# Another order of the loading phase in a fused attention and gated-MLP kernel

## The chip, the cores and the metric

The kernel runs on one core of a Trainium2 chip. The metric is the device time of one execution in microseconds (us); the kernel before takes 225.37 us, the median of three runs (225.3 to 225.51).

## What is computed

```python
def _attn_ref(x, state):                       # x (8, 8, 512, 64), state (8, 8, 32, 64)
    scores = scale * np.matmul(x, state.transpose(0, 1, 3, 2))
    a = softmax(scores)                        # over the 32 states
    xread = np.matmul(a, state)
    scores2 = scale * np.matmul(state, x.transpose(0, 1, 3, 2))
    a2 = softmax(scores2)                      # over the 512 tokens
    sread = np.matmul(a2, x)
    return np.concatenate([xread, sread], axis=2)
# then, with heads and depth as 512 features, for all 8 * 544 tokens:
gate = 1.0 / (1.0 + np.exp(-(y @ w_gate)))     # (512, 1536)
val = y @ w_val
return gate * val @ w_out                      # (1536, 512)
```

## The kernel before

The kernel goes through eight batches. For the tokens of a batch it never forms `xread`: it multiplies the state with the weights first (`sw_visit` for batches 0 and 1, `sw_wide` for the others: the products `SW`, for 256, 512 or 768 of the 1536 columns at a time, for the gate with w = 0 and for the value with w = 1, each in two halves e). Then it multiplies the softmax `a`, transposed, with `SW` (`gv_mm(b, f)`: four matmuls for each of the twelve groups f of 128 columns). ScalarE takes the tanh of the gate half (`gv_th`, L298), VectorE joins the two halves (`gv_glu`, L303), and `out_mm` multiplies with `w_out` (twelve calls of four matmuls a batch). Groups f = 0 and 1 need the columns from 0 on, f = 2 and 3 those from 256 on, f = 4 to 7 those from 512 on, and the rest those from 1024 on.

What leads up to `gv_mm(b, ...)` is the attention part. `load_x` brings x of a batch (pieces of two heads, 256 KB each, for batches 0 and 1), `cast_x` turns it into bf16, `xT_mm` and `xT_cp` transpose two heads (four calls j a batch), `S_mm` and `S_exp` give the exponentials of the scores for half a batch i, `n_sum` (a reduction and a reciprocal, L139 and L141) and `n_mul` the normalised softmax, `aT_mm` and `aT_cp` its transpose. `at_Eb` casts the exponentials to bf16 for the other direction, `sr_mm` and `sr_fin` (L218, L226) form `sread` in `XS`. `sT_mm`, `sT_pad` and `sT_cp` transpose the state, `pad` copies the state of batches 2 to 7 into `sTz`. `sw_cp` (L274) moves one half of one `SW` product from the accumulator banks to SBUF. For batches 2 and later x and the softmax are transposed by DMA (`at_xT_dma`, `aT_dma`), issued on SP's queue.

TensorE writes into eight accumulator banks: two of `GV`, four of `SWP`, one each of `OU` and `AT`. A product must wait until its bank's last reader is done.

Weights are loaded by GpSimd's queue (`load_w`, `load_wo`, cast on the way), in which these issues stand in one line with GpSimd's own casts and products (POOL in the profile). x of batches 0 and 1 is issued on SP's queue.

All of batches 0 and 1 is written out by hand, instruction by instruction, as is the start of batch 2: every call adds its instructions to the queues of its engines in the order of the listing, and every engine does its own queue in order. `warm(n, place)` puts n matmuls of constants into TensorE's queue that nobody reads. From batch 2 on a loop over b and f (L654 to L704) does the same in every batch, with `gv_mm(b, f)` and `out_mm(b - 1, f)` in turn and the attention part of the next batch between them. "The loop" below means this one, and its start is the first matmul of `sw_wide(3, 0)`.

Of the kernel before, what the change touches and what calls it, by code (L numbers as in the profile page):

```python
# [16 lines left out]
def kernel(  # L17
# [465 lines left out]
    aT_mm(1, OU)
    sw_cp(1, 0, 2, 0, act)
    sw_cp(0, 0, 2, 1, act)
    gv_th(0, 3)
    gv_mm(0, 2, SWP)
    sw_cp(0, 0, 2, 0, vec)
    gv_mm(0, 0, SWP)
# [248 lines left out]
```

## Time and profile before

| | us |
|---|---|
| median of three runs | 225.37 |
| the profiled execution | 226.03 |
| its span, first to last instruction | 224.2 |
| outside the span | 1.83 |
| TensorE busy | 217.0 (97%) |
| VectorE busy | 140.7 (63%) |
| ScalarE busy | 127.6 (57%) |
| GpSimd busy | 48.8 (22%) |
| granted clock of TensorE | 1.000 |
| first matmul of `gv_mm(0, 3)`, the first of its kind | 16.40 |
| start of the loop | 56.22 |

PE is TensorE, PEld its weight loads, DVE VectorE, ACT ScalarE, POOL GpSimd, SP SyncE. TensorE's busy time counts the `warm` matmuls too (63 of them, all before 9.7 us). A row of the timeline gives the start and the length of a run of like instructions, and in brackets how long the engine had been idle and who released it. A row of the chain gives only the start, the length and the link of the one path that ended last.

### The profile page before, as it was taken

How to read it: one execution, taken by the hardware profiler on the slowest of the kernel's cores; microseconds unless marked ns; L12 is line 12 of the kernel's file. 1: busy time of each engine (PE TensorE's matmuls, PEld its weight loads, DVE VectorE, ACT ScalarE, POOL GpSimd, SP SyncE). 2: the span in 40 equal slices, each digit the busy share in tenths (PEclk: the TensorE clock that was granted, in tenths of full speed). 3: DMA queues.
4: the chain of work that ended last, by engine and by line, in shares of the span. 5: the costliest groups of instructions: out<-in, count | busy, mean ns of one | idle time of the engine just before them, and what ended most of it. 6: DMA issues, size and time to landing. Idle time of an engine off the chain costs nothing.

```text
span 224.2 us, 4791 instructions
## 1 busy us (share of the span) xinstructions
PE 217.0 (97%) x1859; PEld 111.2 (50%) x1859; DVE 140.7 (63%) x248; ACT 127.6 (57%) x239; POOL 48.8 (22%) x85
## 2 busy tenths in 40 slices
PE   7789999999999999999999999999999999999994
PEld 6654444444444545454444454454445444466744
DVE  3599897779368756885488648864787434422311
ACT  2587885645676557656675667556755444423311
POOL 3799560362041004200240006000200000000001
PEclk9999999999999999999999999999999999999999
DMA  6999989753898352627362521253122111111114
GB/s 188 289 201 206 280 130 179 114 193 78 147 292 274 71 151 76 219 59 126 100 225 50 121 96 61 44 81 117 47 78 66 50 50 47 67 73 48 50 26 114
DMA packets 38566, 27.37 MB, mean 122 GB/s; under 512 B 21168, under 2 KB 33840, under 8 KB 38544
## 3 DMA queue, kind: packets, MB, share of 16 engines
q1 hardware_dynamic: 31392, 19.74, 32.5%
q0 software_dynamic: 6864, 7.14, 17.6%
q8 instruction: 14, 0.23, 0.4%
q10 hardware_dynamic: 288, 0.20, 0.3%
q14 instruction: 8, 0.07, 0.1%
HBM read 18.35 MB, written 8.91 MB: 122 GB/s over the span
## 4 chain that ended last, share of the span: by engine, by line
PE 91%; DVE 3%; DMA 2%; ACT 1%; SPq 1%; issue 0%
PE outp L319 38%; PE gvp L288 37%; PE swp L236 5%; PE gvp L291 5%; DMA xf<-in_x_dram 2%; PE srp L213 1%; PE Sp L121 1%; PE outp L339 1%; DVE rs L139 1%; PE srp L210 1%; SPq L74 1%; DVE ab L173 1%; DVE ri L141 0%; DVE r L218 0%; PE xTp L105 0%; PE warm L353 0%
## 5 line engine op out<-in xcount | busy, mean ns | idle before, releaser
L303 DVE SCALAR_TENSOR_TENSOR glu<-th,gvp 128x512 bf16<-128x512 f32 (+1 forms) x108 | 69.9, 655 | 64.0 <-ACT th L298 48.7
L319 PE MATMUL outp<-wo,glu 128*128 128x512 bf16 x396 | 98.2, 379 | 0.0
L288 PE MATMUL gvp<-aT,SW 128*128 128x512 bf16 x384 | 96.3, 379 | 0.3 <-DVE aT L190 0.2
L298 ACT ACTIVATE th<-gvp 128x512 f32<-128x512 f32 (+1 forms) x108 | 61.8, 574 | 60.6 <-PE gvp L288 49.2
L288 PEld LDWEIGHTS <-SW 128*128 128x128 bf16 x384 | 36.3, 98 | 44.7 <-issue 3.1
L319 PEld LDWEIGHTS <-glu 128*128 128x128 bf16 x396 | 37.4, 98 | 40.8 <-issue 0.4
L274 ACT CAST SW<-swp 128x512 bf16<-128x512 f32 x70 | 38.8, 586 | 4.7 <-PE swp L236 3.3
L132 POOL CAST Eb<-E 128x256 bf16<-128x256 f32 x32 | 11.5, 407 | 89.9 <-ACT E L126 89.9
L323 ACT ACTIVATE res<-outp 128x512 f32<-128x512 f32 x33 | 19.7, 597 | 17.6 <-PE outp L319 17.6
L274 DVE CAST SW<-swp 128x512 bf16<-128x512 f32 x26 | 17.1, 683 | 1.6 <-PE swp L236 1.4
L91 POOL CAST xb<-xf 128x1024 bf16<-128x1024 f32 (+1 forms) x13 | 13.8, 1093 | 12.1 <-DMA xf<-in_x_dram 10.7
L330 POOL DMA_DIRECT2D out_dram<-res x2 | 1.1, 542 | 60.0 <-ACT res L323 60.0
L147 DVE TENSOR_REDUCE E<-E 128x128 f32<-128x512 f32 x12 | 12.4, 1035 | 0.0
L139 DVE TENSOR_REDUCE rs<-E 128x16 f32<-128x512 f32 x16 | 10.8, 676 | 1.3 <-ACT E L126 1.3
L126 ACT ACTIVATE E<-Sp 128x512 f32<-128x512 f32 x16 | 9.6, 604 | 2.4 <-PE Sp L121 2.4
L173 DVE TENSOR_TENSOR ab<-E,ri 128x512 bf16<-128x512 f32 x12 | 9.6, 804 | 0.0
L236 PE MATMUL swp<-wg,sTc 64*32 64x512 bf16 (+1 forms) x192 | 8.4, 328 | 0.0
L236 PEld LDWEIGHTS <-sTc 64*32 64x32 bf16 x384 | 4.5, 91 | 7.4 <-issue 4.7
L218 DVE RECIPROCAL r<-srp 128x128 f32<-128x128 f32 x8 | 7.6, 950 | 0.0
L121 PEld LDWEIGHTS <-xT 128*128 128x128 bf16 x128 | 5.5, 98 | 4.0 <-DVE xT L108 1.0
L236 PE MATMUL swp<-wv,sTc 64*32 64x512 bf16 (+1 forms) x192 | 7.4, 322 | 0.0
L291 PE MATMUL gvp<-XS,wg 128*128 128x256 bf16 x48 | 7.2, 273 | 0.0
(64 smaller groups left out, 122.0 us busy)
## 6 DMA issues: line engine op xcount, KB each, us to landing
out_dram<-res SPq DMA_DIRECT2D x31, 256.0 KB, 2.6
xf<-in_x_dram SPq DMA_DIRECT2D x12, 256.0 KB, 4.5
xf<-in_x_dram SPq DMA_DIRECT2D x3, 1024.0 KB, 6.8
wo<-in_moe_w_out_dram POOLq DMA_DIRECT2D x3, 512.0 KB, 5.9
wg<-in_moe_w_gate_dram POOLq DMA_DIRECT2D x2, 512.0 KB, 9.2
wv<-in_moe_w_val_dram POOLq DMA_DIRECT2D x2, 512.0 KB, 10.8
xf<-in_x_dram POOLq DMA_DIRECT2D x2, 512.0 KB, 10.4
xf<-in_x_dram POOLq DMA_DIRECT2D x1, 1024.0 KB, 9.2
```

The lines of the kernel that those rows point to most:

```text
L91: cp(xbs[b].rearrange("p c h d -> p h c d")[:, lo:lo + n], xfs[b][:, lo:lo + n])
L139: nc.vector.tensor_reduce(rs, halfE(b, i), AX.X, ALU.add)
L147: nc.vector.tensor_reduce(held["E4", b][:, e].rearrange("p j n -> p (j n)"), E1s[b][:, :, e].rearrange("p c j n -> p (j n) c"), AX.X, ALU.add)
L173: eng.tensor_tensor(abs_[b].rearrange("p c e (j n) -> p (c e) j n", n=Ns)[:, ce, 2 * i:2 * i + 2], halfE(b, i)[:, ce], ri[:, ce].unsqueeze ...
L236: nc.tensor.matmul(pss[e][j * Ns:(j + 1) * Ns, o:o + n], sTc[rows, b, j] if b > 1 else sTz[rows, b, j, e], (wg, wv)[w][rows, j, lo:lo + n] ...
L274: cp(*sw_left.pop((b, lo, w, e)))
L288: nc.tensor.matmul(ps, SWs[b][:, g, w, fs], aTs[b][:, :, g], start=(g == 0), stop=(g == 1))
L291: nc.tensor.matmul(ps, (wg, wv)[w][:, j, fs], XS[:, j], start=(j == 0), stop=(j == 3))
L298: nc.scalar.activation(th, held["gv", b, f][0], AF.Tanh, scale=0.5)
L303: nc.vector.scalar_tensor_tensor(glus[b][:, f], held["th", b, f], 1.0, held["gv", b, f][1], ALU.add, ALU.mult)
L319: nc.tensor.matmul(ops[b, c], glus[b][:, f, c * 128:(c + 1) * 128], wo[:, f], start=(f == 0), stop=(f == NF - 1))
L323: nc.scalar.activation(res, ops[b, c], AF.Copy, scale=0.5)
```

## The change

The two `load_x` of batches 0 and 1 at the head become one; x of batch 1 is loaded by `load_xp`, one piece each at its place in the listing, in the order 3, 2, 0, 1. `hold(1, i)` lets GpSimd write one element of piece i before that, so that the piece's load has a write of GpSimd to wait for. Batch 0 is taken from head 0 on: the scores of heads 0 to 3 (i = 0) come before those of heads 4 to 7, where before it was the other way round. The first five `load_w` stand in GpSimd's queue directly behind its casts of the state and of x's first piece; the last three come behind its casts of batch 1. `at_Eb` is split by quarters over VectorE, ScalarE and GpSimd, the casts of x are shared out anew, `n_sum` is split into its two instructions, and the number of `warm` matmuls goes from 63 to 85. The first `gv_mm`, the `sw_visit` and everything up to the loop stand in another order; the loop is the same.

The listing of the new order runs up to the loop, several calls to a line; that of the old one up to the fourth `gv_mm`.

```diff
@@ -73,6 +73,18 @@
         for i in range(parts):
             eng.dma_start(xf[:, n * i:n * i + n], v[:, n * i:n * i + n])
+    def load_xp(b, i):
+
+        if b not in xfs:
+            xfs[b] = stg.tile((128, H, 4, D), FP, name="xf")
+        nc.sync.dma_start(xfs[b][:, 2 * i:2 * i + 2], x[b].rearrange("h (p c) d -> p h c d", c=4)[:, 2 * i:2 * i + 2])
+
+    def hold(b, i):
+
+        if b not in xfs:
+            xfs[b] = stg.tile((128, H, 4, D), FP, name="xf")
+        nc.gpsimd.memset(xfs[b][:, 2 * i, 0, 0:1], 0.0)
+
     def load_w(w, lo, n):
         src = (moe_w_gate, moe_w_val)[w].rearrange("(k p) n -> p k n", p=128)
         nc.gpsimd.dma_start((wg, wv)[w][:, :, lo:lo + n], src[:, :, lo:lo + n])
@@ -120,25 +132,37 @@
             for c in range(4):
                 nc.tensor.matmul(ps[:, c, :, jj], xTs[b][:, 2 * i + jj, c], sTz[:, b, 2 * i + jj], start=True, stop=True)
-    def S_exp(b, i):
+    def S_exp(b, i, lo=0, n=4):
         if b not in E1s:
             E1s[b] = ap_.tile((128, 4, 2, 4, Ns), FP, name="E1")
-        nc.scalar.activation(E1s[b][:, :, :, 2 * i:2 * i + 2].rearrange("p c e j n -> p (c e) j n"),
-                             held["S", b, i].rearrange("p c e j n -> p (c e) j n"), AF.Exp, scale=scale)
+        nc.scalar.activation(halfE(b, i)[:, 2 * lo:2 * lo + 2 * n],
+                             held["S", b, i][:, lo:lo + n].rearrange("p c e j n -> p (c e) j n"), AF.Exp, scale=scale)
+
+    def Eb_c(b, c, cp):
+        if b not in Ebs:
+            Ebs[b] = ap_.tile((128, 4, 2, 4, Ns), BF, name="Eb")
+        cp(Ebs[b][:, c], E1s[b][:, c])
     def at_Eb(b):
-        Ebs[b] = ap_.tile((128, 4, 2, 4, Ns), BF, name="Eb")
         for c in range(4):
-            nc.gpsimd.tensor_copy(Ebs[b][:, c], E1s[b][:, c])
+            Eb_c(b, c, pool)
     def halfE(b, i):
         return E1s[b][:, :, :, 2 * i:2 * i + 2].rearrange("p c e j n -> p (c e) j n")
+    def n_red(b, i, lo=0, n=4):
+        if ("rs", b, i) not in held:
+            held["rs", b, i] = ap_.tile((128, 8, 2), FP, name="rs", bufs=4)
+        nc.vector.tensor_reduce(held["rs", b, i][:, 2 * lo:2 * lo + 2 * n], halfE(b, i)[:, 2 * lo:2 * lo + 2 * n], AX.X, ALU.add)
+
+    def n_rec(b, i, lo=0, n=4):
+        if ("ri", b, i) not in held:
+            held["ri", b, i] = ap_.tile((128, 8, 2), FP, name="ri", bufs=4)
+        nc.vector.reciprocal(held["ri", b, i][:, 2 * lo:2 * lo + 2 * n], held["rs", b, i][:, 2 * lo:2 * lo + 2 * n])
+
     def n_sum(b, i):
-        rs = ap_.tile((128, 8, 2), FP, name="rs")
-        nc.vector.tensor_reduce(rs, halfE(b, i), AX.X, ALU.add)
-        ri = held["ri", b, i] = ap_.tile((128, 8, 2), FP, name="ri")
-        nc.vector.reciprocal(ri, rs)
+        n_red(b, i)
+        n_rec(b, i)
     def n_tok(b, e):
@@ -390,266 +414,285 @@
     sbs = {}
     load_s(0, nc.scalar)
-    load_x(0, nc.sync, 4)
-    load_x(1, nc.sync, 4)
     make_identity(nc, ident)
...
-    nc.vector.memset(sTz, 0.0)
...
+    load_x(0, nc.sync, 4)
+    nc.vector.memset(sTz, 0.0)
...
-   cast_x(0, pool, 0, 2); warm(12, OU); cast_x(0, vec, 2, 2); warm(16, GV); warm(8, OU); cast_s(0, pool)
-   load_w(1, 256, 256); sT_mm(0, OU); sT_pad(0, 1, vec); cast_x(0, act, 6, 2); xT_mm(0, 1, SWP); xT_mm(0, 0, AT)
-   cast_x(0, act, 4, 2); sT_pad(0, 0, vec); warm(15, GV); xT_mm(0, 3, OU); xT_cp(0, 0, vec); load_w(0, 256, 256)
-   warm(3, GV); xT_mm(0, 2, SWP); xT_cp(0, 1, vec); xT_cp(0, 2, vec); xT_cp(0, 3, act); warm(3, GV)
-   load_w(0, 0, 256); cast_x(1, vec, 2, 2); warm(6, GV); gate(xfs[0][:, 7, 0, 0:1]); S_mm(0, 1, SWP, (0,))
-   S_mm(0, 1, OU, (1,)); S_mm(0, 0, OU, (0,)); load_w(1, 0, 256); cast_x(1, act, 0, 2); S_mm(0, 0, AT, (1,))
-   S_exp(0, 1); cast_x(1, vec, 4, 2); n_sum(0, 1); load_w(0, 512, 512); S_exp(0, 0); xT_mm(1, 0, SWP)
-   xT_mm(1, 1, SWP); cast_x(1, pool, 6, 2); at_Eb(0); xT_mm(1, 2, AT); xT_cp(1, 2, vec); n_sum(0, 0)
-   xT_mm(1, 3, OU); xT_cp(1, 3, act); S_mm(1, 1, GV); load_sb(2); xT_cp(1, 0, act); S_exp(1, 1); xT_cp(1, 1, vec)
-   S_mm(1, 0, AT); n_mul(0, 1, nc.vector); n_mul(0, 0, nc.vector); n_sum(1, 1); sw_visit(0, 256, 256); sr_mm(0, OU)
-   S_exp(1, 0); sw_cp(0, 256, 2, 1, act); aT_mm(0, AT); sw_visit(1, 256, 256); sw_cp(0, 256, 2, 0, act)
-   aT_cp(0, 0, act); n_sum(1, 0); sw_visit(1, 0, 256); aT_cp(0, 1, vec); load_w(0, 1024, 512); load_w(1, 512, 512)
-   load_w(1, 1024, 512); n_mul(1, 1, nc.gpsimd); sr_fin(0); sw_cp(1, 0, 2, 1, vec); sw_cp(1, 256, 2, 1, act)
-   gv_mm(0, 3, GV); sw_cp(1, 256, 2, 0, act); sw_visit(0, 0, 256); n_mul(1, 0, nc.gpsimd); aT_mm(1, OU)
-   sw_cp(1, 0, 2, 0, act); sw_cp(0, 0, 2, 1, act); gv_th(0, 3); gv_mm(0, 2, SWP); sw_cp(0, 0, 2, 0, vec)
-   gv_mm(0, 0, SWP); aT_cp(1, 0, vec); gv_th(0, 2); gv_glu(0, 3); gv_mm(0, 1, GV); gv_th(0, 0); gv_glu(0, 2)
-   sT_mm(2, AT); aT_cp(1, 1, vec); gv_glu(0, 0); sw_visit(1, 512, 512, 0); gv_th(0, 1); gv_glu(0, 1)
...
+   warm(16, GV); warm(14, OU); hold(1, 1); cast_x(0, vec, 2, 2); hold(1, 2); hold(1, 3); cast_s(0, pool)
+   sT_mm(0, AT); sT_pad(0, 0, act); sT_pad(0, 1, act); cast_x(0, pool, 0, 2); warm(6, GV); xT_mm(0, 0, SWP)
+   cast_x(0, vec, 4, 2); xT_mm(0, 1, SWP); warm(7, GV); xT_mm(0, 2, GV); xT_cp(0, 1, vec); load_w(0, 256, 256)
+   xT_cp(0, 0, act); load_xp(1, 3); S_mm(0, 0, SWP, (0,)); S_mm(0, 0, AT, (1,)); S_exp(0, 0); cast_x(0, vec, 6, 2)
+   xT_cp(0, 2, vec); load_w(1, 256, 256); warm(3, GV); xT_mm(0, 3, AT); xT_cp(0, 3, vec); n_red(0, 0)
+   load_xp(1, 2); n_rec(0, 0); cast_x(1, act, 6, 2); S_mm(0, 1, SWP, (0,)); warm(5, GV); S_mm(0, 1, OU, (1,))
+   S_exp(0, 1); n_red(0, 1); xT_mm(1, 3, OU); load_w(0, 0, 256); load_w(1, 0, 256); load_w(0, 512, 512)
+   xT_cp(1, 3, act); Eb_c(0, 0, vec); Eb_c(0, 1, vec); n_rec(0, 1); n_mul(0, 1, nc.vector); cast_x(1, pool, 4, 2)
+   warm(6, GV); xT_mm(1, 2, SWP); load_xp(1, 0); cast_x(1, pool, 0, 2); warm(7, GV); xT_mm(1, 0, GV)
+   xT_cp(1, 2, act); Eb_c(0, 3, act); S_mm(1, 1, GV); S_exp(1, 1); n_red(1, 1); n_rec(1, 1); Eb_c(0, 2, pool)
+   sr_mm(0, OU); xT_cp(1, 0, vec); load_xp(1, 1); cast_x(1, pool, 2, 2); xT_mm(1, 1, SWP); xT_cp(1, 1, act)
+   n_mul(0, 0, nc.gpsimd); load_w(1, 512, 512); load_w(0, 1024, 512); load_w(1, 1024, 512); aT_mm(0, AT)
+   aT_cp(0, 0, act); aT_cp(0, 1, vec); warm(6, GV); sw_visit(0, 256, 256); sw_cp(0, 256, 2, 1, vec)
+   sw_visit(1, 256, 256); sw_cp(1, 256, 2, 1, vec); sw_cp(0, 256, 2, 0, act); S_mm(1, 0, GV); S_exp(1, 0)
+   warm(7, AT); gv_mm(0, 3, GV); Eb_c(1, 0, pool); n_red(1, 0); sw_cp(1, 256, 2, 0, act); warm(8, SWP)
+   sw_visit(0, 0, 256); n_rec(1, 0); gv_th(0, 3); gv_glu(0, 3); sw_cp(0, 0, 2, 0, act); sw_cp(0, 0, 2, 1, vec)
+   sr_fin(0); sw_visit(1, 0, 256); gv_mm(0, 2, GV); sw_cp(1, 0, 2, 0, act); gv_mm(0, 0, SWP); gv_th(0, 2)
+   gv_glu(0, 2); n_mul(1, 1, nc.gpsimd); gv_th(0, 0); n_mul(1, 0, nc.gpsimd); aT_mm(1, AT); aT_cp(1, 0, vec)
+   gv_glu(0, 0); sw_cp(1, 0, 2, 1, act); Eb_c(1, 3, act); aT_cp(1, 1, vec); gv_mm(0, 1, GV); gv_th(0, 1)
+   gv_glu(0, 1); sw_visit(1, 512, 512, 0); sw_cp(1, 512, 0, 0, act); load_x(2, nc.gpsimd, 2)
+   sw_cp(1, 512, 0, 1, act); sw_visit(0, 512, 512, 0); sw_cp(0, 512, 0, 1, vec); sw_cp(0, 512, 0, 0, act)
+   gv_mm(1, 3, SWP); load_sb(3); gv_th(1, 3); gv_glu(1, 3); Eb_c(1, 1, pool); gv_mm(1, 0, GV); gv_th(1, 0)
+   p_tok(1); gv_glu(1, 0); sw_visit(1, 512, 512, 1); sw_cp(1, 512, 1, 1, vec); sw_cp(1, 512, 1, 0, act)
+   gv_mm(1, 2, SWP); gv_th(1, 2); gv_glu(1, 2); gv_mm(1, 7, GV); load_sb(1); gv_th(1, 7); gv_glu(1, 7)
+   Eb_c(1, 2, pool); sw_visit(1, 1024, 512, 0); sw_cp(1, 1024, 0, 0, vec); sw_cp(1, 1024, 0, 1, act)
+   sw_visit(0, 1024, 512, 0); sw_cp(0, 1024, 0, 0, act); gv_mm(1, 1, GV); gv_th(1, 1); sr_mm(1, OU)
+   sw_visit(1, 1024, 512, 1); sw_cp(1, 1024, 1, 1, act); sw_cp(0, 1024, 0, 1, vec); sw_cp(1, 1024, 1, 0, act)
+   sw_visit(0, 1024, 512, 1); gv_mm(1, 6, GV); gv_glu(1, 1); sw_cp(0, 1024, 1, 0, vec); sw_cp(0, 1024, 1, 1, act)
+   sr_fin(1); gv_mm(1, 10, SWP); gv_th(1, 10); gv_glu(1, 10); gv_th(1, 6); gv_mm(0, 10, SWP); gv_th(0, 10)
+   gv_glu(1, 6); gv_glu(0, 10); gv_mm(1, 4, SWP); gv_th(1, 4); gv_mm(0, 11, GV); cast_x(2, act, 0, 4); gv_glu(1, 4)
+   sw_visit(0, 512, 512, 1); gv_th(0, 11); gv_glu(0, 11); sT_mm(1, SWP); sT_cp(1, act); load_sb(2)
+   sw_cp(0, 512, 1, 1, act); sT_mm(2, AT); sT_cp(2, vec); load_wo(0); cast_x(2, pool, 4, 4); at_xT_dma(2)
+   load_wo(1); sT_mm(3, OU); sw_cp(0, 512, 1, 0, act); gv_mm(1, 11, SWP); gv_th(1, 11); gv_mm(0, 9, GV)
+   gv_th(0, 9); gv_glu(0, 9); gv_mm(1, 5, SWP); gv_glu(1, 11); gv_th(1, 5); sT_cp(3, act); gv_mm(0, 7, GV)
+   gv_th(0, 7); gv_glu(0, 7); gv_glu(1, 5); gv_mm(0, 5, SWP); gv_mm(1, 8, GV); gv_th(0, 5); gv_th(1, 8)
+   gv_glu(0, 5); gv_glu(1, 8); gv_mm(0, 4, SWP); gv_th(0, 4); gv_glu(0, 4); gv_mm(1, 9, GV); gv_th(1, 9)
+   gv_glu(1, 9); gv_mm(0, 8, SWP); gv_th(0, 8); gv_glu(0, 8); gv_mm(0, 6, GV); gv_th(0, 6); gv_glu(0, 6); pad(2, 6)
+   S_mm(2, 0, SWP); S_exp(2, 0); n_red(2, 0); S_mm(2, 1, GV); S_exp(2, 1); n_rec(2, 0); sw_wide(2, 0)
+   out_mm(0, 7, GV); sw_cp(2, 0, 2, 1, act); sw_cp(2, 0, 0, 0, act); out_mm(0, 0, GV); out_mm(0, 9); sw_wide(2, 1)
+   out_mm(0, 2); load_wo(2); load_x(3, nc.gpsimd); out_mm(0, 1, AT); n_red(2, 1); sw_cp(2, 0, 0, 1, act)
+   n_rec(2, 1); n_mul(2, 1, nc.vector); sw_cp(2, 0, 1, 0, act); gate(xTs[2][:, 0, 3, 0:1]); sw_cp(2, 0, 2, 0, vec)
+   sw_cp(2, 0, 1, 1, act); n_mul(2, 0, nc.gpsimd); out_mm(0, 6, OU); aT_dma(2); at_Eb(2); cast_x(3, pool, 0, 4)
+   cast_x(3, pool, 4, 4); sw_cp(2, 1, 0, 1, vec); sw_cp(2, 1, 0, 0, act); at_xT_dma(3); sw_cp(2, 1, 1, 0, act)
+   out_mm(0, 3); n_tok(2, 0); out_mm(0, 8); sw_cp(2, 1, 2, 1, act); n_tok(2, 1); n_split(2, 0); out_mm(0, 5)
+   load_x(4, nc.sync); out_mm(0, 10); sw_cp(2, 1, 2, 0, act); n_split(2, 1); sr_mm(2, SWP); sw_cp(2, 1, 1, 1, act)
+   sr_fin(2); out_mm(0, 4); out_mm(0, 11)
```

More of the change, by code (lines that the diff above doesn't have):

```diff
@@ L479 @@
-    gv_mm(0, 3, GV)
-    sw_cp(1, 256, 2, 0, act)
-    sw_visit(0, 0, 256)
-    n_mul(1, 0, nc.gpsimd)
[L483 to L489, printed above, removed]
+    warm(16, GV)
+    warm(14, OU)
+    hold(1, 1)
+    cast_x(0, vec, 2, 2)
+    hold(1, 2)
+    hold(1, 3)
+    cast_s(0, pool)
+    sT_mm(0, AT)
+    sT_pad(0, 0, act)
+    sT_pad(0, 1, act)
+    cast_x(0, pool, 0, 2)
+    warm(6, GV)
@@ new lines @@
+    n_red(1, 1)
+    n_rec(1, 1)
+    Eb_c(0, 2, pool)
+    sr_mm(0, OU)
+    xT_cp(1, 0, vec)
+    load_xp(1, 1)
+    cast_x(1, pool, 2, 2)
+    xT_mm(1, 1, SWP)
+    xT_cp(1, 1, act)
+    n_mul(0, 0, nc.gpsimd)
+    load_w(1, 512, 512)
+    load_w(0, 1024, 512)
+    load_w(1, 1024, 512)
+    aT_mm(0, AT)
+    aT_cp(0, 0, act)
+    aT_cp(0, 1, vec)
+    warm(6, GV)
+    sw_visit(0, 256, 256)
+    sw_cp(0, 256, 2, 1, vec)
+    sw_visit(1, 256, 256)
+    sw_cp(1, 256, 2, 1, vec)
+    sw_cp(0, 256, 2, 0, act)
@@ L505 @@
[L505 to L523 removed]
+    sw_cp(0, 512, 0, 1, vec)
+    sw_cp(0, 512, 0, 0, act)
+    gv_mm(1, 3, SWP)
@@ L580 @@
     gv_th(1, 4)
[L581 to L590 removed]
+    gv_mm(0, 11, GV)
+    cast_x(2, act, 0, 4)
+    gv_glu(1, 4)
+    sw_visit(0, 512, 512, 1)
+    gv_th(0, 11)
+    gv_glu(0, 11)
+    sT_mm(1, SWP)
+    sT_cp(1, act)
+    load_sb(2)
+    sw_cp(0, 512, 1, 1, act)
+    sT_mm(2, AT)
+    sT_cp(2, vec)
+    load_wo(0)
+    cast_x(2, pool, 4, 4)
```

375 lines of the change are left out of this document (179 added, 196 removed).

## Prediction

> **What bounds the kernel now.** I read the shares of busy time first, then the chain of waits, then the timelines of TensorE and VectorE over the first 60 us, and last the DMA queues in the stretch in which x lands. The page's chain names TensorE for 91% of the span, so a change in the loading phase is worth what it does to the start of the loop: behind it TensorE has no idle time that a different past could fill.
>
> ```profile
> PE 91%; DVE 3%; DMA 2%; ACT 1%; SPq 1%; issue 0%
> ...
> 2.27 5.24 DMA xf<-in_x_dram
> 7.53 0.63 ACT xb L91
> ...
> 16.03 0.32 DVE aT L190
> 16.35 0.88 DVE r L218
> ...
> 18.50 2.62 PE gvp L288 x12
> ...
> 56.29 0.77 PE swp L236 x32
> ```
>
> In the chain, the last piece of x of batch 0 lands at 7.51. From there the path runs over ScalarE and then nearly without a break over VectorE to 17.85, then over TensorE to the end. The timeline of TensorE gives the two marks that I use:
>
> ```profile
> 16.40 1.02 PE L288 MATMUL gvp<-aT,SW 128*128 128x512 bf16 x4 [0.18 <-DVE aT L190]
> 18.34 2.78 PE L288 MATMUL gvp<-aT,SW 128*128 128x512 bf16 x12
> 21.05 0.32 PE L374 MATMUL stp<-ident,sb 128*64 128x64 bf16 x8
> ```
>
> The first gv_mm starts at 16.40, the fourth is done at 21.05, and from there to the loop's start at 56.22 no wait for another engine of more than 0.1 us is listed. Those 35.2 us are pure TensorE work, and the kernel after has the same work there. So its loop starts at (end of its fourth gv_mm) + 35.2 + (new waits).
>
> **Prices.** From the timelines: 12 matmuls of gv_mm in 2.62, so 0.87 for a gv_mm; two sw_visit of 512 columns in 0.83; ScalarE moves a bank in 0.60 alone and 0.53 in a row, VectorE in 0.64; a glu takes 0.64, the reduction and the reciprocal of n_sum 0.68 and 0.25, sr_fin 1.5 (the two rows here). TensorE's result reaches the next engine 0.2 to 0.25 us after its last matmul was issued (S_mm left TensorE at 9.88, ScalarE began at 10.09), and a result of ScalarE or VectorE reaches TensorE after 0.06.
>
> ```profile
> 16.27 0.95 DVE L218 RECIPROCAL r<-srp 128x128 f32<-128x128 f32 x1
> 17.25 0.59 DVE L226 TENSOR_TENSOR XS<-srp,r 64x128 bf16<-64x128 f32 x2
> 17.88 1.29 DVE L274 CAST SW<-swp 128x512 bf16<-128x512 f32 x2
> 19.52 1.28 DVE L303 SCALAR_TENSOR_TENSOR glu<-th,gvp 128x512 bf16<-128x512 f32 x2
> 27.96 1.07 ACT L274 CAST SW<-swp 128x512 bf16<-128x512 f32 x2 [0.20 <-PE swp L236]
> ```
>
> **x of batch 1 released by pieces: nothing.** GpSimd is idle from 1.30 to 4.22, so its three one-column writes (rows of such writes: 0.09 each) are done by 1.6. SP needs 0.5 per issue and comes to batch 1's first piece at 2.7. The new wait has been met by then; behind it only the other three pieces are queued. All eight pieces are issued when they were before, batch 1's in another order. I keep the landings: batch 0's last at 7.53, batch 1's at about 8.3, 9.0, 9.7 and 10.36 (first and second worked out from the median of 5.4 us to landing of these eight, the last from GpSimd's row).
>
> **Five weight loads ahead: nothing.** They leave GpSimd from 4.85 to 8.6 instead of 5.12 to 9.17. But the engines are not free for them:
>
> ```profile
> q1 hardware_dynamic: 1333, 1.28, 94.6%
> q0 software_dynamic: 90, 0.05, 8.9%
> ```
>
> This is the DMA view from 5 to 9 us: 1333 packets of x (q1), 90 of weights (q0), with four weight loads issued. Weights begin to flow when x is through, near 9, at 200 GB/s, and keep that rate to 24; so each load lands by its place in the line. The two of 256 columns that come first land by 12.9, the fourth at 15.9 (TensorE's row of a wait for wv at 15.92), the last of the eight near 26. Walked below, they are asked for at 13.8, 16.9 and 28.7: no wait. If that cover went, 1 us of lateness of the fourth load would cost about 1 us. The last three loads stand behind GpSimd's casts and its n_mul (1.04) and go out from 12.3 instead of 13.1: nothing either, by the same line. The Trainium skill's page "DMA: Bandwidth & Descriptors", section "Queues, rings and completion order", says that an engine takes packets in turn from the queue rows that have work. By that rule loads issued 0.27 earlier would take half of that, 0.13 us, from x's last piece, and the sum would be 0.13 higher; the 1333 packets against 90 do not agree with it.
>
> **The chain to the first gv_mm.** From 7.53 VectorE casts batch 0's last piece (0.54), copies two transposes (8.43; TensorE transposes heads 6 and 7 between; 8.95) and sums heads 0 to 3 (9.88). ScalarE has S_exp(0, 1) done at 10.05, then two copies of transposes (10.55, 11.1), a quarter of Eb (11.45) and S_exp(1, 1) (12.4). The casts of Eb on VectorE and ScalarE are not in the trace; the nearest rows are 0.28 (L165, VectorE, same shape) and 0.37 (L377, ScalarE), bounds 0.25 and 0.6; VectorE has 0.4 us spare there, ScalarE none, so its one can cost -0.1 to +0.25. TensorE does sr_mm(0) to 12.5, the last transposes and aT_mm(0) to 13.3; ScalarE copies to 14.1, VectorE follows to 14.55 and moves one half of each of the first two sw_visit (15.2, 15.85). gv_mm(0, 3) starts at 15.35, 1.05 earlier than before. Its second half waits for S_exp(1, 0), whose bank it takes (15.7), and it ends at 16.2.
>
> **From there to the fourth gv_mm.** Before, sw_visit(1, 0) came ahead of the first gv_mm; now it comes behind, with sw_visit(0, 0) and eight warm matmuls: 17.45. gv_mm(0, 2) and (0, 0) follow to 19.2, aT_mm(1) to 19.7. VectorE has meanwhile n_sum(1, 0), a glu, one SW half and sr_fin(0) in its queue, to 19.65, and the glu that frees the bank for gv_mm(0, 1) ends at 20.3. The fourth gv_mm ends at 20.8. The lead has shrunk from 1.05 to 0.25.
>
> **New waits up to the loop**, each a bank not yet read:
> - sw_visit(0, 512) for glu(0, 0), which stands behind aT_cp on VectorE (21.35): 0.15.
> - gv_mm(1, 3) takes the two banks of sw_visit(1, 512); ScalarE moves them from 21.45 to 22.55 (2 x 0.55) and TensorE is there at 21.75: 0.3 + 0.1. Before, gv_mm(1, 0) in other banks stood at this place.
> - gv_mm(1, 7) for the SW half that VectorE moves last: 0.05; gv_mm(1, 4) for th(0, 10): 0.15.
> - S_mm(2, 1) for th(0, 6), sw_wide(2, 0) and (2, 1) for single banks: 0.15, 0.05 and 0.1.
>
> Sum 1.05. Against the lead of 0.25 the loop starts 0.8 us later, at 57.0. The other gv_mm come in turn in GV and SWP with th and glu shorter than 0.87, so they hide theirs. The extra warm matmuls (22 at 0.067, as 15 in 1.00) lie in stretches where TensorE waits anyway, but for the eight in front of sw_visit(0, 0), 0.5, which are in the walk.
>
> **The sum.** The profiled execution is 224.2 + 1.83 = 226.03 and lies 0.66 over the median 225.37. I add the shift to the median: 225.37 + 0.8 = 226.2 (for a profiled execution like that of before, 226.8). A measurement of this kernel can tell about 0.2%, 0.45 us, from no change.
>
> **Rivals.**
> 1. Faster: VectorE catches up. All waits above but the one for th(0, 10) go back to VectorE and ScalarE being 0.2 to 0.6 us behind TensorE from 19 to 22.5, and the bounds of my walk are of that size. If the walk is 0.35 too slow up to the first gv_mm and VectorE reaches sr_fin(0) 0.4 earlier as well, the lead stays at 0.6 and no wait is left: 224.8. For it: the first gv_mm really starts earlier. Against: VectorE is over 95% busy from 11 to 24 us already now, and TensorE has 0.85 more in front of its fourth gv_mm. It decides if the glu of (0, 2) ends before 19.7. Chance 0.17.
> 2. No change: the hold does hold. If batch 1's pieces stayed out of x's way, batch 0's four (1.05 MB at 345 GB/s) would land near 6.5, and the chain would run 0.9 earlier, until it meets the weight load at 15.9: 225.3. Against: the idle GpSimd row. With what the forecast's own spread puts there, chance 0.16.
> 3. Slower still: x of batch 3 comes late. pad waits for sT_cp(3), which ScalarE now does near 38.3; behind pad (1.72) GpSimd issues load_wo(2) and load_x(3), at 40.9 instead of 40.14. It lands 9.7 later as now, the casts take 2.03, the four transposes of SP 6.16, and the last lands 2.2 later: 61.4. The loop asks for them 4.24 after its start (before, 60.46 against 56.22), at 61.2. That is on the edge, and the forecast counts nothing for it. Every later landing costs its full amount; with 1 us, 227.2. It decides if load_x(3) goes out after 41. Chance 0.17.
>
> **How the numbers follow.** Forecast 0.50, rivals 0.17, 0.16, 0.17. Slower by over 0.45 us: forecast and the third, 0.67; within: 0.16; faster: 0.17. The forecast's own range is 225.8 to 227.2 (waits of half or twice their size, the ScalarE cast's bounds). The whole range goes from the first rival, 224.7, to the third with doubled waits, 227.2 + 0.7 = 227.9.
>
> **What would show it.** In the profile after: SP's eight issues of x without a gap; weights landing as before; gv_mm(0, 3) near 15.4 and the fourth gv_mm ending near 20.8; idle gaps in TensorE's rows ahead of gv_mm(0, 1) and gv_mm(1, 3), released by VectorE and ScalarE; the loop's start near 57.0. It is wrong if the loop starts before 56 or if TensorE stands still for over 0.5 us at any place not named here.

## The result

The kernel after takes 227.10 us (median of 13 runs, 225.72 to 228.35), the kernel before beside it 225.45 (13 runs, 225.17 to 226.16): 1.0067 times as long, 95% interval 1.0042 to 1.0092. Forecast: 226.2 in a range from 224.7 to 227.9, slower with a chance of 0.67. Sign and range held, the time lies inside the forecast's own range of 225.8 to 227.2 too; the size, 0.8, was about half of the 1.65 that was measured.

The first thing to see is that the two profiled executions cannot simply be subtracted: 226.19 for after is among its shortest, 226.03 for before among its longest, and they differ by 0.16 us where the medians differ by 1.65. So the rows below show what the kernel after does in one of its shorter executions, not the whole of what it loses. The page's chain and TensorE's timeline of after, as in the prediction for before:

```profile
PE 91%; DVE 3%; DMA 2%; issue 1%; SPq 1%; ACT 1%
```

```profile
15.15 1.03 PE L312 MATMUL gvp<-aT,SW 128*128 128x512 bf16 x4
...
20.18 0.59 PE L312 MATMUL gvp<-aT,SW 128*128 128x512 bf16 x2 [0.28 <-DVE glu L327]
20.70 0.81 PE L260 MATMUL swp<-wg,sTz 64*32 64x512 bf16 x16
21.82 1.51 PE L312 MATMUL gvp<-aT,SW 128*128 128x512 bf16 x6 [0.30 <-ACT SW L298]
...
56.36 0.41 PE L260 MATMUL swp<-wg,sTc 64*32 64x512 bf16 x8
```

In this execution nearly all is where the prediction put it: the first gv_mm at 15.15 (forecast 15.35), the fourth done at 20.70 (20.8), the wait for VectorE's glu before gv_mm(0, 1), the wait for ScalarE's SW half before gv_mm(1, 3). The loop starts at 56.36 (57.0). The loads, too, do what was said. SP's issues of x follow each other without a gap, and from 5 to 9 us the engines carry 1305 packets of x (q1) and 44 of weights (q0):

```profile
0.74 1.99 SPq L74 DMA_DIRECT2D xf<-in_x_dram  x4
2.78 2.00 SPq L80 DMA_DIRECT2D xf<-in_x_dram  x4
```

```profile
q1 hardware_dynamic: 1305, 1.26, 99.3%
q0 software_dynamic: 44, 0.02, 4.2%
```

The chain over the start shows one thing that the prediction did not have, two VectorE links longer than they were priced: two casts of Eb in 0.82, priced at 0.28 each, and n_mul, the row that writes `ab`, in 1.27 instead of 0.65:

```profile
9.92 0.69 DVE rs L156
10.60 0.82 DVE Eb L144 x2
11.42 0.17 DVE ri L161
11.61 1.27 DVE ab L197
```

### The profile page after: what moved, and what is told of

The parts are those of the page before. It is cut to its first block, busy times and chain, and to the rows that moved or that the text cites. A ratio compares the mean times of both kernels' runs of the same rounds, so it can differ in the third digit from the quotient of the medians.

```text
span 224.4 us, 4813 instructions
## 1 busy us (share of the span) xinstructions
PE 217.2 (97%) x1857; PEld 112.8 (50%) x1881; DVE 139.1 (62%) x240; ACT 131.7 (59%) x249; POOL 49.2 (22%) x84
## 4 chain that ended last, share of the span: by engine, by line
PE 91%; DVE 3%; DMA 2%; issue 1%; SPq 1%; ACT 1%
PE outp L343 37%; PE gvp L312 37%; PE swp L260 5%; PE gvp L315 5%; DMA xf<-in_x_dram 2%; PE Sp L133 2%; PE srp L237 1%; PE outp L363 1%; PE srp L234 1%; PE warm L377 1%; SPq L74 1%; DVE glu L327 1%; DVE ab L197 1%; DVE r L242 0%; DVE Eb L144 0%
## 5 line engine op out<-in xcount | busy, mean ns | idle before, releaser
L343 PE MATMUL outp<-wo,glu 128*128 128x512 bf16 x372 | 95.0, 379 | 1.1
L298 ACT CAST SW<-swp 128x512 bf16<-128x512 f32 x76 | 42.0, 587 | 4.2 <-PE swp L260 2.8
L144 POOL CAST Eb<-E 128x256 bf16<-128x256 f32 x28 | 10.8, 426 | 92.2 <-ACT E L138 92.2
L103 POOL CAST xb<-xf 128x1024 bf16<-128x1024 f32 (+1 forms) x15 | 15.1, 1033 | 6.0 <-DMA xf<-in_x_dram 6.0
L298 DVE CAST SW<-swp 128x512 bf16<-128x512 f32 x20 | 13.5, 684 | 0.4 <-PE swp L260 0.2
L197 DVE TENSOR_TENSOR ab<-E,ri 128x512 bf16<-128x512 f32 x12 | 10.4, 869 | 0.1
L377 PE MATMUL warm<-ones 128*128 128x128 bf16 x85 | 8.2, 259 | 1.0 <-DVE ones L420 1.0
```

The source lines that it names most:

```text
L103: cp(xbs[b].rearrange("p c h d -> p h c d")[:, lo:lo + n], xfs[b][:, lo:lo + n])
L144: cp(Ebs[b][:, c], E1s[b][:, c])
L197: eng.tensor_tensor(abs_[b].rearrange("p c e (j n) -> p (c e) j n", n=Ns)[:, ce, 2 * i:2 * i + 2], halfE(b, i)[:, ce], ri[:, ce].unsqueeze ...
L298: cp(*sw_left.pop((b, lo, w, e)))
L343: nc.tensor.matmul(ops[b, c], glus[b][:, f, c * 128:(c + 1) * 128], wo[:, f], start=(f == 0), stop=(f == NF - 1))
```

## The experiments

Marks of every profiled execution, in us: the first gv_mm; the end of the fourth (start of the next row on TensorE); the start of the loop; what lies behind it to the end of the span; and how long after the loop's start SP issues the first store of the loop's results. Ratios are to the kernel before, measured beside it on the same chip. e1 to e4, e5 to e8, e9 to e11 and e12 ran on four different chips, so across these groups it is the ratios that compare.

| kernel | median | ratio, 95% interval | first gv_mm | fourth done | loop | behind | store |
|---|---|---|---|---|---|---|---|
| before, first profile | 225.45 | 1 | 16.40 | 21.05 | 56.22 | 168.0 | 2.14 |
| before, again | one run, 225.02 | | 15.81 | 20.26 | 55.20 | 168.0 | 2.13 |
| after, first profile | 227.10 | 1.0067, 1.0042 to 1.0092 | 15.15 | 20.70 | 56.36 | 168.0 | 1.26 |
| after, again (e1) | 227.78 | 1.0104, 1.0072 to 1.0136 | 15.79 | 21.34 | 57.00 | 168.0 | 1.47 |
| e3 before's start | 226.48 | 1.0045, 1.0025 to 1.0065 | 16.11 | 20.75 | 56.34 | 168.7 | 1.97 |
| e4 after's start | 227.29 | 1.0076, 1.0053 to 1.0099 | 15.80 | 21.36 | 56.74 | 169.1 | 1.56 |
| e5 Eb off VectorE | 226.25 | 1.0036, 1.0015 to 1.0056 | 15.09 | 20.65 | 56.24 | 168.2 | 1.49 |
| e6 n_mul on VectorE | 226.01 | 1.0029, 1.0004 to 1.0054 | 14.77 | 20.33 | 55.92 | 168.0 | 1.43 |
| e7 no hold | 227.78 | 1.0120, 1.0076 to 1.0163 | 15.95 | 21.51 | 57.17 | 168.9 | 2.35 |
| e8 both of e5, e6 | 226.26 | 1.0040, 1.0019 to 1.0061 | 14.58 | 20.13 | 55.72 | 168.4 | 1.64 |
| e9 behind gv_mm only | 226.53 | 1.0048, 1.0030 to 1.0065 | 15.47 | 20.39 | 56.60 | 168.4 | 1.79 |
| e10 e6 and e9 | 226.66 | 1.0051, 1.0028 to 1.0074 | 14.72 | 19.65 | 55.79 | 169.1 | 2.78 |
| e12 e10, VectorE relieved | 225.79 | 1.0006, 0.9992 to 1.0021 | 14.84 | 19.76 | 55.40 | 169.0 | 2.51 |

**Both kernels again (e1, e2), unchanged.**

> The kernel after once more, unchanged, for a second profiled execution and more times. Theory A (the loading phase itself scatters: landings of x or of weights reach TensorE unhidden, so slow executions lose time ahead of the fourth gv_mm): if this profiled execution is over 226.7 us, its fourth gv_mm ends later than the 20.70 us of the first profile by most of the excess. Theory B (the bank waits between the fourth gv_mm and the loop are what scatters): the fourth gv_mm ends near 20.7 in a slow execution too, and the loop starts later than 56.4. Theory C (the loop itself loses: x of batch 3 or the clock of TensorE): the loop starts near 56.4 and the excess lies behind it, or the granted clock falls below 1. Times: 225.7 to 228.4, median near 227.1, in all three.

> The kernel before once more, for a second profiled execution: its first one took 226.03 us, 0.58 over the median of its runs. All theories: a time of 225.2 to 226.2; if it is near 225.4, first gv_mm and loop start stand up to 0.6 us earlier than the 16.40 and 56.22 of the first profile, which then were late ones.

The two spans now differ by 1.8 us (225.0 and 223.2), all of it ahead of the loop. This execution of before, at 225.02 a little under what was expected, has x's last piece of batch 0 about 1 us earlier than the first one had (its cast begins at 6.51 instead of 7.53). e1 took 227.04, 0.85 more than the first profile of after, and 0.64 of that stands at the end of the fourth gv_mm. That is the place that theory A names, but not its reason: x's last piece is cast from 7.13 on in e1 and from 7.25 in the first profile, and no wait for a weight is listed. Instead sr_mm(0), the product that writes `srp`, stands still; the waits of TensorE, then VectorE's and GpSimd's timelines of e1:

```profile
PE srp L234 <- DVE Eb L144: 1.1, 1, 1.1
```

```profile
9.75 0.69 DVE L156 TENSOR_REDUCE rs<-E 128x16 f32<-128x512 f32 x1
10.35 2.13 DVE L144 CAST Eb<-E 128x256 bf16<-128x256 f32 x2
12.41 0.24 DVE L161 RECIPROCAL ri<-rs 128x16 f32<-128x16 f32 x1
12.68 0.69 DVE L197 TENSOR_TENSOR ab<-E,ri 128x512 bf16<-128x512 f32 x1
```

```profile
10.12 0.44 POOL L144 CAST Eb<-E 128x256 bf16<-128x256 f32 x1
10.47 0.65 POOL L103 CAST xb<-xf 128x512 bf16<-128x512 f32 x1
11.05 1.07 POOL L197 TENSOR_TENSOR ab<-E,ri 128x512 bf16<-128x512 f32 x1
12.05 0.81 POOL L90 DMA_DIRECT2D wv<-in_moe_w_val_dram  x1
```

Of the two casts of Eb on VectorE the one took 1.93 us and the other 0.28. The long one ends at 12.28, 0.16 behind the end of GpSimd's row of three instructions, when only weight issues are left; n_mul behind it then takes its normal 0.69. The profiles of e7 and e9, further down, repeat this: a cast of 2.16 that ends 0.16 behind the end of GpSimd's n_mul, and one of 2.47 that ends 0.17 behind it. In the first profile of after it was the other way round: the casts 0.90 for both, and n_mul, beside GpSimd's own n_mul, 1.26. For comparison VectorE's products and GpSimd's work in the first profile of before, where the casts of Eb are all GpSimd's and over before VectorE's products begin:

```profile
13.03 1.28 DVE L173 TENSOR_TENSOR ab<-E,ri 128x512 bf16<-128x512 f32 x2
```

```profile
11.23 1.44 POOL L132 CAST Eb<-E 128x256 bf16<-128x256 f32 x4 [0.23 <-ACT E L126]
...
13.13 0.75 POOL L78 DMA_DIRECT2D wg<-in_moe_w_gate_dram  x1
13.86 1.50 POOL L78 DMA_DIRECT2D wv<-in_moe_w_val_dram  x2
```

What it costs when an instruction of VectorE is caught, that is, made longer by GpSimd's, can be counted from the start of VectorE's second reduction, n_red(0, 1), to the first gv_mm: 5.23 in the first profile of after, where n_mul was caught, 6.04, 6.26 and 6.58 in e1, e7 and e9, where a cast was, and 5.24 to 5.42 in the profiles of e6, e10 and e12, where GpSimd's n_mul is gone. So a cast that is caught for the whole row costs 0.6 to 1.0 us in e1 and e7 (in e9 VectorE came to it early and stood still for longer), and n_mul caught as in the first profile costs nothing that shows.

**One half of the change each (e3, e4).** e3 has before's order up to the fourth gv_mm and after's from there to the loop; e4 the reverse.

```diff
 e3: the calls up to gv_glu(0, 1) from the kernel before (without load_sb(2), sT_mm(2)), the rest from after
     (with Eb_c(1, 0) and Eb_c(1, 3) on GpSimd, which after has further ahead)
 e4: the calls up to gv_glu(0, 1) from the kernel after (with load_sb(2)), the rest from before
```

> The order of before up to the fourth gv_mm (with state load and transpose of batches 4 and 5 left to the later place), then the order of after up to the loop. Theory A (loading phase): 225.3 to 225.9, and little scatter like before's. Theory B (bank waits behind the fourth gv_mm, +0.5 to +1.05 us): 226.0 to 226.6. Theory C (x of batch 3 issued later, a part of this half): above 226.5 with the scatter of after.

> The order of after up to the fourth gv_mm (with one 64 KB state load added behind GpSimd's product), then the order of before up to the loop. Theory A (loading phase): 226.5 to 227.2 with runs spread over 2 us, like after. Theory B: 225.0 to 225.3, since the start alone is 0.25 to 0.35 us ahead by the walk and by the profile. Theory C: 225.0 to 225.4.

Each half costs time, after's start (e4) more than after's rest (e3). e3 is where theory B puts it, e4 0.1 us over the range of theory A. e4 shows the wait of TensorE for VectorE's Eb that e1 has, at 0.8 us instead of 1.1. e3 loses 0.4 to 0.65 us between the fourth gv_mm and the loop (35.59, before 35.17 and 34.94) and 0.7 behind the loop's start. e4 loses 1.1 there. Its last 16 us ran at a granted clock of 0.97 (0.99 and 1.00 in after and before), by an estimate from these figures 0.3 to 0.5 us of that; what the rest was stays open.

**What VectorE and GpSimd do to each other (e5, e6, e8), and the named parts undone (e7).** Theory A: VectorE's casts and products from SBUF to SBUF (the chip's on-chip memory) stand still while GpSimd's instructions run. Theory B: the scatter comes from the landing of x.

```diff
 e5 (e8 has this and e6)
-    Eb_c(0, 0, vec)
-    Eb_c(0, 1, vec)
...
-    Eb_c(0, 3, act)
+    Eb_c(0, 0, act)
+    Eb_c(0, 1, act)
...
     Eb_c(0, 2, pool)
+    Eb_c(0, 3, pool)
 e6
     n_mul(0, 1, nc.vector)
+    n_mul(0, 0, nc.vector)
...
-    n_mul(0, 0, nc.gpsimd)
 e7
-    hold(1, 1)
-    hold(1, 2)
-    hold(1, 3)
...
+    gate(xfs[0][:, 7, 0, 0:1])
     load_w(1, 0, 256)
     load_w(0, 512, 512)
```

> The kernel after, with the two casts of Eb that stand on VectorE (Eb_c(0, 0) and Eb_c(0, 1)) given to ScalarE, and ScalarE's own (0, 3) to GpSimd. Theory A (VectorE's casts from SBUF to SBUF stand still while GpSimd's instructions run: 0.28 us where GpSimd is idle, 1.93 in one execution): no wait of TensorE for VectorE's Eb any more, sr_mm(0) starts at 11.2 to 11.6, but n_mul(0, 1) on VectorE still meets GpSimd's n_mul(0, 0) (1.26 instead of 0.65); first gv_mm at 15.1 to 15.4 in every execution, the median 0.3 to 0.8 us below the kernel after as it was run twice (227.10, 227.78), so 226.5 to 227.0, with less scatter. Theory B (the scatter comes from the landing of x's pieces): median 227.1 to 227.8 and the same scatter of 2 us; the first gv_mm moves with the landing.

> The kernel after, with n_mul(0, 0) moved from GpSimd to VectorE, behind n_mul(0, 1). Theory A: GpSimd has no long instruction left between its cast of x at 10.5 and its weight issues, so a VectorE cast that was caught behind both of GpSimd's instructions is now caught behind the cast alone, and is done by 11.4 at the latest; the two n_mul take 0.65 each; aT_mm(0) starts near 12.9 to 13.1 instead of 13.0 to 13.8; first gv_mm 14.9 to 15.3; time 226.3 to 226.9. Theory B: 227.1 to 227.8. If instead VectorE's queue is what counts, the 0.65 us that it gets in addition make the first gv_mm 0.3 to 0.6 later, 227.5 and above.

> The kernel after without the change's named parts: no hold (GpSimd's three writes into x of batch 1 are left out, so its pieces wait for nothing), and the last two of the five weight loads held back behind the landing of x's last piece of batch 0, as before. Forecast of the prediction (both parts cost and bring nothing): 227.1 to 227.8, as the kernel after in two earlier measurements. Rival: the five loads ahead of the casts push GpSimd's casts into VectorE's, so that GpSimd's work moves by some 0.5 us and with it which of the two loses: then the median moves by 0.3 us or more either way, and VectorE's Eb casts show another length than 1.93.

> Both edits: the casts of Eb off VectorE (two on ScalarE, two on GpSimd) and n_mul(0, 0) on VectorE. Theory A: nothing of VectorE that GpSimd can stop is left from 10 to 13 us but n_mul(0, 1) against GpSimd's cast of x; first gv_mm at 14.8 to 15.2, little scatter, the fourth gv_mm ends at 20.4 to 20.7, time 226.0 to 226.6, still above the kernel before by the waits behind the fourth gv_mm. Theory B: 227.1 to 227.8.

e5, e6 and e8 have medians 0.8 to 1.8 us below the two measurements of after, and 1.5 to 1.8 below e7, which was measured beside them and is where after is: theory A in the main. Not all of it came as forecast. e5 and e6 are 0.25 and 0.3 us faster than their ranges, the two edits together (e8) are worth no more than one of them, and the runs of e5 and e8 still spread over 1.7 and 1.8 us (after 2.6). VectorE in e6, then VectorE and the end of GpSimd's row in e5, and the waits of TensorE in e7:

```profile
9.98 1.11 DVE L144 CAST Eb<-E 128x256 bf16<-128x256 f32 x2
11.01 0.24 DVE L161 RECIPROCAL ri<-rs 128x16 f32<-128x16 f32 x1
11.28 1.29 DVE L197 TENSOR_TENSOR ab<-E,ri 128x512 bf16<-128x512 f32 x2
```

```profile
10.00 2.81 DVE L197 TENSOR_TENSOR ab<-E,ri 128x512 bf16<-128x512 f32 x1
```

```profile
11.20 1.05 POOL L197 TENSOR_TENSOR ab<-E,ri 128x512 bf16<-128x512 f32 x1
```

```profile
PE srp L234 <- DVE Eb L144: 1.1, 1, 1.1
```

With n_mul(0, 0) away from GpSimd, VectorE's two products take 0.65 each, and it does one more of them and is still done earlier. In e5 the casts are gone from VectorE and the stall has moved to n_mul: one of 0.65 takes 2.81, from 10.0 until 0.56 behind the end of GpSimd's row of casts and its n_mul. TensorE waits 0.5 for it.

Theory B is not wholly out: over all profiles the cast of x's last piece begins between 6.51 and 7.54, whatever the kernel. In the profiles of e5, e6 and e8 it begins at 6.65 to 6.75, in after, e1 and e7 at 7.12 to 7.25, and the second reduction 0.3 to 0.9 earlier with it. None of the edits stands ahead of that cast, so this is no part of their gain. Between e1 and e6 it makes 0.37 of the 1.0 us at the fourth gv_mm (the reduction begins at 9.75 and 9.38) and leaves 0.65. In e5 the stretch from the reduction to the first gv_mm is as long as in e1 (6.09 and 6.04), and that its edit gains is shown by its median alone. e7 shows no gain from leaving out the hold and moving the last two of the five loads; the intervals of 0.3 to 0.4% to either side would hide an effect of half a us.

**The disputed cost by itself (e11).** The kernel before with six stretches behind its end.

```diff
+    start(); v_cast(4)                                            # VectorE alone
+    start(); p_cast(6); v_cast(4)                                 # beside GpSimd's casts
+    start(); p_cast(6); n_mul(z, 1, nc.vector) x3; v_cast(4)
+    start(); p_cast(6); n_sum(z, 1); n_sum(z, 0); v_cast(4)
+    start(); load_w(0, 256 * k, 256) for k in range(4); v_cast(4)
+    start(); v_cast(4); p_cast(4)
```

> The kernel before with a trial of VectorE beside GpSimd added behind its last output; its time is longer by the trial and says nothing. Six stretches, in each of which VectorE does four casts of Eb's size (128x256, float32 to bfloat16): alone; beside six of GpSimd's casts of x in a row; the same behind three n_mul; the same behind two n_sum; beside four weight loads issued by GpSimd; and VectorE first, GpSimd's casts behind. Theory A (one of the two stands still while the other's instruction runs): 0.28 us each when alone; beside six casts of 0.6 us a cast or n_mul of VectorE takes 0.6 to 3.6 us, up to the end of GpSimd's row if it loses each turn; n_sum takes its usual 0.68 and 0.25, as it did beside GpSimd in the kernel after. Rival (the two share and both get slower by a part): VectorE's casts all take the same 0.4 to 0.6 and GpSimd's casts get longer by as much.

VectorE's timeline, and GpSimd's beside the second and the third stretch:

```profile
220.83 0.89 DVE L718 CAST Eb<-E 128x256 bf16<-128x256 f32 x4
...
222.14 2.52 DVE L718 CAST Eb<-E 128x256 bf16<-128x256 f32 x4
...
225.96 2.98 DVE L173 TENSOR_TENSOR ab<-E,ri 128x512 bf16<-128x512 f32 x3
...
231.33 0.68 DVE L139 TENSOR_REDUCE rs<-E 128x16 f32<-128x512 f32 x1
232.04 0.25 DVE L141 RECIPROCAL ri<-rs 128x16 f32<-128x16 f32 x1
...
235.38 1.14 DVE L718 CAST Eb<-E 128x256 bf16<-128x256 f32 x4
...
238.96 2.57 DVE L718 CAST Eb<-E 128x256 bf16<-128x256 f32 x4
```

```profile
222.06 3.62 POOL L714 CAST xb<-xf 128x512 bf16<-128x512 f32 x6
...
225.75 4.88 POOL L714 CAST xb<-xf 128x512 bf16<-128x512 f32 x6
```

Four casts take 0.89 alone and 2.52 beside GpSimd's casts: one of VectorE's for each of GpSimd's, 0.69 each where they took 0.28. n_mul takes 0.98 instead of 0.65 and GpSimd's casts 1.07 instead of 0.61. The reduction and the reciprocal keep their 0.68 and 0.25, and in the stretch with the weight issues (the row at 235.38) only the last of four casts is longer (0.53). So it is neither the even sharing of the rival nor, here, the loss of every turn: the two go in turns, one for one. In the last stretch (238.96) one of the four casts took 1.14, two turns. Why a cast lost a whole row of three in e1, and n_mul in e5, the trial does not show; it has no product on GpSimd, and in the kernel the row ends with one.

**The waits behind the first gv_mm (e9, e10, e12).** e9 is after with the three edits below, e10 has them and e6's, e12 is e10 with the last two.

```diff
 e9, e10
-    warm(8, SWP)
...
-    sr_fin(0)                 # ahead of gv_glu(0, 2)
...
+    sr_fin(0)                 # behind gv_glu(0, 1)
...
+    gv_mm(1, 0, GV)           # from behind gv_mm(1, 3)
+    gv_th(1, 0)
     gv_mm(1, 3, SWP)
 e12 against e10
-    sr_fin(0)                 # behind gv_glu(0, 1)
     sw_cp(0, 512, 0, 1, vec)
+    sr_inv(0)
...
+    sr_fin(0)                 # behind gv_glu(1, 3)
     sw_visit(1, 512, 512, 1)
-    sw_cp(1, 512, 1, 1, vec)
+    sw_cp(1, 512, 1, 1, act)
```

> The kernel after, with three edits behind the first gv_mm alone: the eight warm matmuls in front of sw_visit(0, 0) left out, sr_fin(0) moved on VectorE from in front of glu(0, 2) to behind glu(0, 1), and gv_mm(1, 0) put ahead of gv_mm(1, 3), as in the kernel before. The prediction's walk: the waits of gv_mm(0, 1) for VectorE's glu (0.28) and of gv_mm(1, 3) for ScalarE's SW half (0.30) go, and the 0.54 of warm matmuls with them: the fourth gv_mm ends 0.8 and the loop starts 1.1 us earlier, counted from the first gv_mm; the collisions of VectorE and GpSimd ahead of it stay. 227.1 to 227.8 less 1.1: 226.0 to 226.7. Rival: VectorE is the limit whatever the order (glu, n_sum, SW halves), and the waits come back in other places: gain 0.3 or less.

> The kernel e6 (n_mul(0, 0) on VectorE) with the three edits of e9. If the two causes are apart, they add up: 226.0 less 1.1 is 224.9, 0.3 below the kernel before; first gv_mm at 14.8, fourth done at 19.5, loop at 54.8. Rival: the waits come back elsewhere, since TensorE is 0.8 us further ahead of VectorE and ScalarE: 225.4 to 226.0, not below the kernel before.

> The kernel e10 with VectorE relieved where e10 showed TensorE's weight loads waiting for VectorE's SW halves (0.9 us in three waits, from 20 to 25.4 us): sr_fin(0) no longer in front of the SW half of sw_visit(0, 512) but its reciprocal behind that half and its two products behind glu(1, 3), and the SW half (1, 512, 1, 1) given to ScalarE. If sr_fin's place is what cost e10 the 0.55 us between the fourth gv_mm and the loop (36.14 against 35.59 in e6), that stretch is now 35.2 to 35.6 and the loop starts at 54.9 to 55.3. What the time is then depends on SP: if its eight transposes are done by 2.2 us after the loop's start (as in e6 and in the second profile of before), 168.0 lie behind the loop, 224.9 in all, as fast as before or faster by 0.3; if they take 12.2 as in e10 instead of 10.9, the stores behind them come late, ScalarE waits for a free result buffer (0.8 in e10) and the time is 225.7 to 226.3. Rival: VectorE's whole queue is the limit, not sr_fin's place; then the stretch stays at 36.0 or more and the time at 226.3 to 226.8.

e9 is inside its forecast with 226.53, but not for its reason. From the first to the end of the fourth gv_mm it takes 4.92 instead of e1's 5.55, 0.6 less where 0.8 was forecast; from there to the loop it takes 36.21 instead of 35.66, and from the first gv_mm to the loop 41.13, against 41.21 in both profiles of after: 0.1 less where 1.1 was forecast. That is what its rival said. e10 is 1.8 us over its forecast and 0.7 over its rival. The fourth gv_mm is done at 19.65, as expected, and no wait of a matmul is listed from there to the loop; yet this stretch takes 36.14 instead of e6's 35.59. The list of waits from 15 to 27 us shows why, in the rows of the weight loads:

```profile
PEld L260 <- issue: 2.2, 7, 0.4
PEld L312 <- issue: 1.7, 6, 0.4
...
PEld L312 <- DVE SW L298: 0.9, 3, 0.5
```

A matmul's row is 0.379 long while the next starts 0.217 later, so up to 0.16 of a stop between two of them shows in no matmul's row, and what TensorE waited for stands at the weight load: VectorE's SW halves, behind sr_fin(0) at its new place. e9 has the same 0.9 in this row, e6 0.2. With the two edits of e12 it is 0.4 and the stretch 35.64 again; which of the two did it was not run apart. And then, at the loop, a second loss, in e10 and e12; the waits of e10, and SP's timeline of e6, e10 and e12:

```profile
ACT res L347 <- DMA out_dram<-res: 1.6, 2, 1.2
...
PE outp L343 <- ACT res L347: 0.8, 1, 0.8
```

```profile
51.42 5.83 SPq L125 DMA_TRANSPOSE xT<-xb  x4
57.35 0.52 SPq L349 DMA_DIRECT2D out_dram<-res  x1
```

```profile
46.15 6.03 SPq L218 DMA_TRANSPOSE aT<-ab  x4
52.28 6.18 SPq L125 DMA_TRANSPOSE xT<-xb  x4
58.57 0.52 SPq L349 DMA_DIRECT2D out_dram<-res  x1
```

```profile
57.91 0.52 SPq L349 DMA_DIRECT2D out_dram<-res  x1
```

The store of the first results stands on SP's queue behind the eight transposes of batches 2 and 3. While it waits, ScalarE finds no free `res` buffer and TensorE no free bank. In the table, the seven executions with after's rest (after, e1, e3, e5 to e8) and e9, e10 and e12 line up: stores 1.26 to 1.49 after the loop's start leave 168.0 to 168.2 behind it, 1.64 gives 168.4, 1.79 gives 168.4, 1.97 gives 168.7, 2.35 gives 168.9, 2.51 and 2.78 give 169.0 and 169.1. So with after's rest a store that comes more than about 1.5 us behind the loop's start costs most of its further lateness. This is read from the waits and the marks; no run moved the store by itself. It does not hold for before's rest: there the store comes 2.13 and 2.14 behind the loop's start and 168.0 us lie behind it all the same, and e4, at 1.56, has 169.1. The transposes themselves take 10.7 to 12.2 us from one execution to another. e12 ends at 225.79, in the second branch of its forecast and not to be told from the kernel before: the change can be mended, but nothing here beats the kernel before.

## Why the prediction was right, and where not

**x by pieces, weight loads: nothing. Right.** No gap on SP, no wait for a weight in after, and e7 without the hold and with two loads held back is no faster (1.0120 against 1.0067 and 1.0104). The rule of the Trainium skill cited there ("DMA: Bandwidth & Descriptors", "Queues, rings and completion order") would have given x's packets and the weights' like numbers as soon as both are queued. That the packets disagree with it, as the prediction says, goes too far: all 44 weight packets of after run between 8 and 9 us, though the first load is issued at 4.51, and the trace does not show from when on they were queued. Nothing of the rule's 0.13 us can be seen.

**The chain to the first gv_mm: 15.35. The step that failed.** The prediction priced VectorE's casts of Eb from a row of another cast at 51.95, when GpSimd was all but idle, 0.28 with an upper bound of 0.6, gave them 0.4 us to spare, and kept n_mul at 0.65. Measured: 1.93 for one cast (e1), 2.36 for both (e7), 1.26 for n_mul (first profile), beside GpSimd's casts and its n_mul, which the change puts at the same time. In the kernel before, Eb is cast by GpSimd alone and VectorE's n_mul meet only weight issues. The rule is in the Trainium skill, "SBUF — State Buffer", section "Who interferes with whom": a copy or a cast of VectorE can need a pair of SBUF ports that GpSimd uses, which one of the two then holds for its whole instruction while the other stands still; an operation with two inputs in SBUF contends with GpSimd's reads; and on this chip reductions never contend. For which operations collide the trace agrees (cast 0.69, n_mul 0.98, reduction unchanged at 0.68, in e11); that one holds it for the whole instruction is more than e11 shows, where a pair, one cast of each engine, went through every 0.61 us, no longer than GpSimd's cast takes alone. The price by the profiles is the 0.6 to 1.0 us up to the first gv_mm where a cast is caught; e6, which takes GpSimd's n_mul away, has a median 1.1 to 1.8 us lower.

**The lead of 0.25 at the fourth gv_mm.** It was taken against 21.05 of a late execution of before. Against the other profile, 20.26, neither profile of after has a lead, and e6, free of most of the collisions, is level with it (20.33). The late one was late by x's landing: from the first cast of x's last piece to the end of the fourth gv_mm before takes 13.5 and 13.75 us, after 13.45 and, with a cast caught (e1), 14.2. The start of the new order as such gives TensorE's first gv_mm 1.0 us earlier (14.77 against 15.81) and all of it is lost by the fourth, as the prediction had it: sw_visit, the warm matmuls and VectorE's queue in front of the glu.

**New waits of 1.05.** Too much, and the 35.2 us they were added to were not pure TensorE work. The prediction looked at the rows of matmuls; at the weight loads the first profile of before lists 0.4 us of waiting for one of VectorE's SW halves in this stretch, and the second profile is through it in 34.94. From the fourth gv_mm to the loop after takes 35.66, before 35.17 and 34.94: 0.5 to 0.7. The 0.3 for gv_mm(1, 3) is there to the digit, as is the one of 0.28 for the glu; of the smaller ones the profile shows none as a row of its own, and in the medians they are part of what e3 costs (1.0045).

**The sum.** 225.37 + 0.8 against a measured + 1.65. That the time lies in the range is in part luck, for the terms failed in both directions: waits counted 0.35 to 0.55 too high, the lead up to 0.8 too high for a typical execution of before, the collisions not at all. With e1's end of the fourth gv_mm, 21.34 instead of 20.8, the sum is 0.8 - 0.45 + 0.4 (half of the 0.8) + 0.55, or 1.3. The rest of the 1.65 is in no profile of after: both profiled executions are shorter than the median of their runs, by 0.9 and 0.7 us. e7's lies at its median (227.99 and 227.78); it has the fourth gv_mm done at 21.51 and 0.9 more behind the loop's start, with the store late. Whether a typical execution of after loses there too stays open.

**Rivals.** 1, VectorE catches up: it did not, and e10 shows what it would have met. 2, the hold holds: it does not, SP's issues of batch 1 follow without a gap, and e7 is no faster without it. No run shows what pieces of batch 1 that stay out of the way would bring. 3 was close to something real: x of batch 3 is not late (its load goes out at 39.71, not 40.9), but the store behind its transposes on the same queue is, by the waits, what stops a loop that comes early (e10, e12) or meets slow transposes (e7).

## What to carry to other kernels

A VectorE cast or product between SBUF operands is priced with what GpSimd does at that moment: if a row of GpSimd's casts lies beside it, count one turn of GpSimd's for each, as in e11, and as an upper bound the whole row, as in e1, e7 and e9; put VectorE's reductions there instead, give the casts to ScalarE (e5), or take GpSimd's product out of the row (e6). A mark of one profiled execution is no baseline for an effect below 1 us: the two of before differ by 0.8 at the fourth gv_mm. Profile the kernel before a second time, and see how far each profile lies from the median of its runs. When TensorE gains, look at its weight loads' waits as well as the matmuls', and at the first store on a queue that carries long transposes.
